# Written order through the last attention chunk, later routing, a third plane buffer, and one load issued from ScalarE, in a fused attention and mixture-of-experts kernel

## The chip, the cores and the metric

The kernel runs on one core of a Trainium2 chip. The metric is the device time of one execution in microseconds; three runs of the kernel before gave 1425.99, 1426.38 and 1427.35 us, so the median is 1426.38 us.

## The reference

For each of 8 batches of 1856 rows, attention without a softmax, multiplied by `u`; the 14848 rows that come out go through a mixture of 16 experts (4 groups of 4), of which each row visits one.

```python
scores = (1.0 / S) * np.matmul(z, z.transpose(0, 2, 1))    # z: 8 x 1856 x 64
attn = np.maximum(scores, 0.0) ** 2
x = (u * np.matmul(attn, v)).reshape(B * S, D)             # D = 256
...
g_idx = np.argmax(x @ w_group, axis=1)                     # a group of four
e_idx = np.argmax(xg @ w_expert[g], axis=1)                # an expert in it
h = np.maximum(xg[mask_e] @ w1[g, e], 0.0)                 # 256 -> 1024
out[tok_idx] = (g_w * e_w)[:, None] * (h @ w2[g, e])       # 1024 -> 256
```

## The kernel before

**Attention.** A batch is cut into four chunks of queries (512, 512, 512 and 320 columns in the batches that matter here), and a chunk into 15 steps, one for each block of 128 keys. The steps of the whole kernel are numbered s = 0 to 479; batch 7, the last, has steps 420 to 479, its third chunk is 450 to 464 and its fourth, the last of all, 465 to 479. I write (7,2) for the third chunk of batch 7, counting from 0. In every turn of the main loop (`for s in range(NS)`) the kernel writes, in this order: loads and splits of operands that are due, `scores(s + 6)`, `attn_v(s)`, at a chunk's last step `chunk_end(s)`, then the deferred work that is due (`run_deferred`), then a few instructions of routing (`run_gens`). `scores` makes the two operands `ah` and `al` of a step, high and low part of the squared scores; `attn_v` is six matmuls on them. So the operands are written six steps ahead of their use.

The score matrix of a batch is symmetric. A key block that an earlier chunk has computed transposed is not computed again: `put_mirror` stores it to DRAM (`sym`), `load_mirror` brings four blocks back into one tile `at` (three buffers) with four DMAs on SyncE's queue, seven steps ahead, and `scores` only splits it: a ScalarE copy `ah<-at` (line 359) and a VectorE subtraction `al<-at,ah` (line 360). In the last chunk 12 of 15 blocks come that way, in three loads; the other three (keys 12 to 14) are computed.

**The end of a chunk.** `chunk_end` multiplies the sums by `u` into `xT` (one buffer), splits `xT` into `xh` (ScalarE, `split_x`) and `xl` (VectorE, `rest_x`), copies it as 16-bit planes into `pl` (`planes`, ScalarE, line 465), from which four DMA transposes on SyncE's queue make rows, computes the router's logits (four matmuls `pl<-xh,whl` and `pl<-xl,wh`, lines 483 and 484) and brings these through `lgp` and a DMA transpose to `lgx`. Each piece is due a number of steps after the chunk: `XO` for the split, `LG` for the logits, `PL` for the planes. `pl` has two buffers (line 116), which `load_x` also uses for the rows that an expert reads back (`xp`).

**Routing.** `route` is a generator of small dependent VectorE instructions for two chunks together, or for one chunk each at the end: 12 or 13 of them lead to a pair of small matmuls (`pk`, lines 610 and 611) that rank the rows by expert; from these come the row addresses `di`, and one indirect DMA on GpSimd's queue per 128 rows scatters the rows to `bucket` in DRAM. The generators run one after the other, 5 instructions a step in the last chunk and 4 a turn behind it. A `yield` with a number waits so many steps. `wait` (line 507) says how long after its chunk a route starts: 15 for chunks (7,0) and (7,1) together, 8 for (7,2), 5 for (7,3). Four times in a route an instruction is wrapped in `pin`: it may not be placed ahead of what its engine was given just before in the written order. One of the pinned ones is the first `pk` matmul.

**Experts.** Expert blocks 0 and 1 are the first 512 rows of two experts and read rows that were scattered long before. A block is `phase1` (48 matmuls, eight groups of six) and `phase2_t` (48 matmuls). Between the groups of blocks 0 and 1, `early` runs one turn of the deferred work and of the routing: eight turns in `phase1`, two in `phase2_t`. After `phase1` of block 1, `while deferred or gens: early(i)` writes out all that is left. Block 2 reads rows that the last scatters write: its load `xp<-bucket` waits for all of them, then `join_x` makes `xf`, `xh_m`, `xl_m`.

**Order.** Instructions are put in order on each engine by a planner with its own model of time, which takes the written order as priority among what it holds ready. Between steps 15 and 465 a region holds TensorE, ScalarE and VectorE to the written order; behind it the planner is free. SyncE and GpSimd are the planner's throughout this stretch.

```python
def early(i):
    run_deferred(late["at"])
    run_gens(late["at"], 4)
    late["at"] += 1
    more_rows(i)
...
pin(nc.tensor.matmul(pk[:, 0:W], tri, ohf, start=True, stop=True))
```

## Time and profile before

| | us |
|---|---|
| median of three runs | 1426.38 |
| the profiled execution | 1423.95 |
| its span, first to last instruction | 1422.1 |
| TensorE busy | 1411.9 |
| VectorE busy | 1216.5 |
| ScalarE busy | 1051.3 |

The span is what one execution's instructions cover; the profiled execution's own time is 1.85 us more. A busy TensorE here is one with a matmul in its pipeline; whether the next matmul came as soon as it could is read from the distances between the starts in the timeline. Names in a row are the tiles of the program, out<-in.

### The profile page before, as it was taken

How to read it: one execution, taken by the hardware profiler on the slowest of the kernel's cores; microseconds unless marked ns; L12 is line 12 of the kernel's file. 1: busy time of each engine (PE TensorE's matmuls, PEld its weight loads, DVE VectorE, ACT ScalarE, POOL GpSimd, SP SyncE). 2: the span in 40 equal slices, each digit the busy share in tenths (PEclk: the TensorE clock that was granted, in tenths of full speed). 3: DMA queues.
4: the chain of work that ended last, by engine and by line, in shares of the span. 5: the costliest groups of instructions: out<-in, count | busy, mean ns of one | idle time of the engine just before them, and what ended most of it. 6: DMA issues, size and time to landing. Idle time of an engine off the chain costs nothing.

```text
span 1422.1 us, 22589 instructions
## 1 busy us (share of the span) xinstructions
PE 1411.9 (99%) x7010; PEld 1223.8 (86%) x7010; DVE 1216.5 (86%) x2436; ACT 1051.3 (74%) x1849; POOL 439.0 (31%) x462
## 2 busy tenths in 40 slices
PE   9999999999999999999999999999999999999998
PEld 7898888888888888888878898988888888899997
DVE  7889999899998999998988667789777888888884
ACT  8887887787887878878776354357777777777773
POOL 0002022220222012202222331332445555555554
PEclk9999999999999999999999999999999999999999
DMA  9997979979899698895987564534555444555552
GB/s 318 328 260 210 235 187 254 230 192 239 195 262 238 160 264 207 223 244 151 243 197 165 116 142 113 122 82 130 126 136 132 126 123 113 138 137 136 139 140 60
DMA packets 400043, 256.47 MB, mean 180 GB/s; under 512 B 244131, under 2 KB 355262, under 8 KB 399920
## 3 DMA queue, kind: packets, MB, share of 16 engines
q1 hardware_dynamic: 387984, 223.97, 63.1%
q0 software_dynamic: 11856, 30.90, 7.7%
q8 instruction: 56, 0.92, 0.3%
q14 instruction: 67, 0.55, 0.1%
q10 hardware_dynamic: 80, 0.13, 0.0%
HBM read 108.29 MB, written 89.21 MB: 139 GB/s over the span
## 4 chain that ended last, share of the span: by engine, by line
PE 92%; DVE 2%; DMA 2%; issue 2%; POOL 1%; ACT 1%; SPq 0%; POOLq 0%; DVEq 0%; ACTq 0%
PE o L408 38%; PE duo_p L887 15%; PE yT L887 6%; PE duo_y L1333 6%; PE sc L370 5%; PE sc L371 5%; PE ph L802 2%; PE ph L803 2%; PE ph L804 2%; PE duo_w L1333 2%; PE duo_x L1333 2%; PE duo_p L1333 2%; PE duo_z L1333 2%; PE pl L483 1%; PE pl L484 1%
## 5 line engine op out<-in xcount | busy, mean ns | idle before, releaser
L408 PE MATMUL o<-ah,vl 128*128 128x512 f32 (+2 forms) x960 | 354.6, 370 | 0.4 <-DVE ah L382 0.4
L408 PE MATMUL o<-ah,vh 128*128 128x512 f32 (+2 forms) x960 | 354.2, 369 | 0.0
L408 PE MATMUL o<-al,vh 128*128 128x512 f32 (+2 forms) x896 | 328.7, 369 | 0.9 <-DVE al L360 0.9
L646 POOL DMA_INDIRECT bucket<-rows,di x121 | 138.6, 1145 | 383.3 <-issue 216.7
L374 ACT ACTIVATE r<-sc 128x512 f32<-128x512 f32 (+2 forms) x312 | 178.8, 573 | 74.4 <-PE sc L371 72.8
L408 PEld LDWEIGHTS o<-ah,vl 128*128 128x128 f32 x960 | 180.2, 188 | 31.0 <-DVE ah L382 1.2
L408 PEld LDWEIGHTS o<-ah,vh 128*128 128x128 f32 x960 | 180.2, 188 | 28.9
L385 DVE TENSOR_TENSOR al<-r,ah 128x512 fp32r<-128x512 f32 (+2 forms) x280 | 187.7, 671 | 19.1 <-ACT r L379 2.2
L930 POOL DMA_INDIRECT out_dram<-y_w,meta_w x92 | 139.3, 1514 | 191.4 <-ACT y_w L924 145.8
L408 PEld LDWEIGHTS o<-al,vh 128*128 128x128 f32 x896 | 167.8, 188 | 27.5 <-DVE al L360 1.2
L887 PE MATMUL duo_p<-hh_w,duo_w 128*128 128x496 f32 (+10 forms) x692 | 178.0, 371 | 0.0
L381 ACT ACTIVATE r<-r 128x512 f32<-128x512 f32 (+2 forms) x280 | 171.4, 612 | 8.9
L887 PEld LDWEIGHTS duo_p<-hh_w,duo_w 128*128 128x128 f32 x692 | 128.6, 188 | 16.7
L382 DVE CAST ah<-r 128x512 fp32r<-128x512 f32 (+2 forms) x280 | 115.9, 414 | 18.8 <-ACT r L381 13.4
L370 PE MATMUL sc<-zm,z2h 128*128 128x512 f32 (+2 forms) x312 | 120.0, 385 | 0.2 <-DVE zm L251 0.2
L371 PE MATMUL sc<-zm,z2l 128*128 128x512 f32 (+2 forms) x312 | 118.9, 381 | 0.0
L310 DVE STREAM_TRANSPOSE mt<-r 128x512 f32<-128x512 f32 x147 | 103.6, 705 | 0.6
L887 PE MATMUL duo_p<-hl_w,duo_w 128*128 128x496 f32 (+10 forms) x346 | 104.1, 371 | 0.0
L360 DVE TENSOR_TENSOR al<-at,ah 128x512 fp32r<-128x512 f32 (+1 forms) x168 | 95.3, 579 | 2.5 <-ACT ah L359 2.3
L359 ACT CAST ah<-at 128x512 fp32r<-128x512 f32 (+1 forms) x168 | 86.1, 531 | 8.8 <-DMA at<-sym 3.9
L807 ACT ACTIVATE hh<-ph 128x512 fp32r<-128x512 f32 (+6 forms) x96 | 45.7, 488 | 39.4 <-PE ph L804 38.6
L887 PE MATMUL yT<-hh,w_e 128*128 128x512 f32 (+6 forms) x352 | 74.1, 328 | 0.0
(259 smaller groups left out, 2874.5 us busy)
## 6 DMA issues: line engine op xcount, KB each, us to landing
sym<-mt SPq DMA_DIRECT2D x126, 256.0 KB
duo_r<-in_w_dram SPq DMA_DIRECT2D x48, 512.0 KB
at<-sym SPq DMA_DIRECT2D x84, 256.0 KB
bucket<-padrow SPq DMA_DIRECT2D x32, 660.0 KB
at<-sym SPq DMA_DIRECT2D x84, 160.0 KB
vr<-in_v_dram SPq DMA_DIRECT2D x23, 512.0 KB
ut<-in_uT_dram SPq DMA_DIRECT2D x23, 512.0 KB
raw_e<-in_w_dram SPq DMA_DIRECT2D x16, 512.0 KB
```

What stands on the lines that cost most here:

```text
L310: nc.vector.transpose(out=t2.rearrange("p (j t x) -> p t j x", t=KT, x=32), in_=a.rearrange("p (t j x) -> p t j x", t=KT, x=32))
L370: held(nc.tensor.matmul(ps[:, 0:w], z2h[:, ks], zm, start=True, stop=False))
L371: held(nc.tensor.matmul(ps[:, 0:w], z2l[:, ks], zm, start=False, stop=True))
L374: held(nc.scalar.activation(out=a, in_=ps[:, 0:w], func=AF.Relu, scale=1.0 / S))
L381: held(nc.scalar.activation(out=a, in_=a, func=AF.Square))
L382: held(nc.vector.tensor_copy(out=ah, in_=a))
L385: held(nc.vector.tensor_sub(out=al, in0=a, in1=f32(ah)))
L408: held(nc.tensor.matmul(oa[d][:, 0:QW[b][c]], (vh if q else vl)[:, d0:d0 + P], al if q == 2 else ah, start=(i == 0 and q == 0), stop=end a ...
L646: nc.gpsimd.indirect_dma_start(out=views[(b * NQ + 2 * half + hs[h]) * NT + i], out_offset=bass.IndirectOffsetOnAxis(ap=di[0:n, i0 + i:i0 ...
L887: nc.tensor.matmul(o, wt["2"][f // 2][:, w0:w0 + P], hs[f][q // 2][:, c0:c0 + n], start=(at == 0), stop=(at == 3 * NF - 1))
L930: nc.gpsimd.indirect_dma_start(out=outs(), out_offset=bass.IndirectOffsetOnAxis(ap=meta[0:m, t, 1:2], axis=0), in_=y[0:m], in_offset=None, ...
L1333: nc.tensor.matmul(out, a, b, start=(q == 0 and m in (1, 5)), stop=(q == 2), skip_group_check=True)
```

## The change

- `pl` has three buffers instead of two.
- The last of the three loads of the last chunk, `(7, 2, 3)`, is issued from ScalarE's queue instead of SyncE's.
- The last chunk takes its keys in another order: 12 and 14 come two steps and one step later, 3 a step earlier, 13 a step later.
- The region of written order ends at step 479 instead of 465. With it, `not last` takes the place of `s + 1 < NS - NK` for chunk (7,2): its split comes 2 steps after the chunk instead of at once, its planes 3 and 4 instead of 1 and 2, its logits 9 instead of 2.
- Logits of chunk (7,1) come 9 steps after the chunk instead of 7; planes stay at 9. The split of (7,0) comes one step sooner.
- The route of (7,0) and (7,1) starts 23 steps after (7,1) instead of 15: at step 472 instead of 464.
- Weight pieces of expert 0 are loaded and split in the order 0, 1, 2, 3, the last two later. The rows of block 0 are loaded three steps later and joined three steps later.
- In the last expert's second half, one output tile has a buffer of its own; the others share `y`.

```diff
--- before.py
+++ after.py
@@ -113,7 +113,7 @@
         return sb("rows", [P, 4, RW], I32, 4, name)
 
     def new_pl(name):
-        return sb("pl", [P, 2048], U16, 2, name)
+        return sb("pl", [P, 2048], U16, 3, name)
 
     def new_xhl(name):
         return tuple(new_vb(f"{h}_{name}").rearrange("p (d q) -> p d q", d=ND) for h in ("xh", "xl"))
@@ -321,9 +321,10 @@
 
         g = QW[b][cc] // 32
         at = new_at(f"at_{b}_{c}_{cc}").rearrange("p (g x) -> p g x", x=P)
+        eng = nc.scalar if (b, c, cc) == (B - 1, 2, NQ - 1) else nc.sync
         src = sym.pop((b, c, cc))[0:g * 32, :].rearrange("(g r) (j x) -> j r g x", r=32, x=P)
         for j in range(4):
-            nc.sync.dma_start(at[j * 32:(j + 1) * 32, 0:g, :], src[j])
+            eng.dma_start(at[j * 32:(j + 1) * 32, 0:g, :], src[j])
         ats[(b, c, cc)] = at[:, 0:g, :].rearrange("p g (t x) -> p t g x", t=KT)
 
     steps = [(b, c, i) for b in range(B) for c in range(NQ) for i in range(NK)]
@@ -336,7 +337,7 @@
 
     def key(b, c, i):
         if (b, c) == (B - 1, NQ - 1):
-            return (0, 1, 12, 2, 3, 14, 4, 5, 13, 6, 7, 8, 9, 10, 11)[i]
+            return (0, 1, 2, 3, 12, 4, 14, 5, 6, 13, 7, 8, 9, 10, 11)[i]
         return KORD[c][i] if MB[0] <= b < MB[1] else i
 
     NS = len(steps)
@@ -495,16 +496,16 @@
                 lgx.rearrange("p t h l -> p (t h) l"), lgp[:, 0:nt].rearrange("p t h q -> p (t h q)")
             )
 
-        LG = (7 if b == B - 1 and c < 2 else (9 if c == 2 else 8 if c == 0 else 7)) if s + 1 < NS - NK else 2
-        XO = 2 if s + 1 < NS - NK else 0
+        LG = (7 + 2 * c if b == B - 1 and c < 2 else (9 if c == 2 else 8 if c == 0 else 7)) if not last else 2
+        XO = (1 if (b, c) == (B - 1, 0) else 2) if not last else 0
         (split_x() if XO == 0 else defer(s + XO, split_x))
         (rest_x() if XO == 0 else defer(s + XO + 1, rest_x))
-        PL = XO + 1 if not XO or c == 2 else LG + 2
+        PL = XO + 1 if not XO or c == 2 else LG + (0 if (b, c) == (B - 1, 1) else 2)
         defer(s + PL, lambda: planes(0))
         defer(s + PL + 1, lambda: planes(1))
         defer(s + LG, logits)
         defer(s + LG + (1 if XO else 0), logits_out)
-        wait = 5 if last else 12 if b == 0 and c < 2 else (17 if c == 1 and b < B - 1 else 15) if s + 1 < NS - NK else 8
+        wait = 5 if last else 12 if b == 0 and c < 2 else (17 if c == 1 and b < B - 1 else 23 if b == B - 1 else 15) if s + 1 < NS - NK else 8
         alone = b == B - 1 and c >= NQ - 2
         if c % 2 or alone:
             gens.append((max(s + wait, PFILL[-1] + 2), route(b, c // 2, (c % 2,) if alone else (0, 1))))
@@ -839,7 +840,7 @@
             for f in range(0 if pair else NF):
                 w2t = wt["2"][f // 2][:, (f % 2) * 512:(f % 2 + 1) * 512]
                 held(nc.tensor.matmul(py[0:m, 0:D], hs[f][1][:, ts], w2t[:, 0:D], start=False, stop=(f == NF - 1)))
-            y = sb("yl", [P, D], F32, 3, f"y_{name}_{t}")
+            y = sb(*(("yl", [P, D], F32, 1) if one else ("y", [P, D], F32, 3)), f"y_{name}_{t}")
             cw = meta[0:m, t, 0:1].bitcast(F32)
             top = py[0:m, 0:D]
             if pair:
@@ -987,7 +988,7 @@
             s0 = (b - 1) * NQ * NK
             begin.setdefault(s0 + load[0] * NK + load[1], []).append((what, b, n))
             split_at.setdefault(s0 + cut[0] * NK + cut[1], []).append((what, b, n))
-    WPREP = ((2, (2, 3), (2, 9)), (0, (2, 4), (2, 12)), (1, (2, 5), (2, 14)), (3, (3, 0), (3, 6)))
+    WPREP = ((0, (2, 3), (2, 12)), (1, (2, 4), (2, 14)), (2, (2, 5), (3, 2)), (3, (3, 6), (3, 11)))
     xs = []
     ahead = 4
     for s in range(ahead):
@@ -1002,7 +1003,7 @@
         b, c, k = steps[s]
         if s == NK:
             region.enter_context(tc.manual_schedule(engines={mybir.EngineType.PE, mybir.EngineType.Activation, mybir.EngineType.DVE}))
-        if s == NS - NK:
+        if s == NS - 1:
             region.close()
         if s in (1, 4):
             pz.pop(0)()
@@ -1029,11 +1030,11 @@
             prep.pop((what, n))()
         if k == (5 if s < NK else 5) and nxt < B * NQ:
             prep_zm(nxt // NQ, nxt % NQ)
-        if s == NS - NK - 6:
+        if s == NS - NK - 3:
             load_rows(0)
         if s == NS - 6:
             load_rows(1)
-        if s == NS - 12:
+        if s == NS - 9:
             xs.append(join_x(0, rows_b[0][0], blocks[0][2]))
         while ahead < min(NS, s + LEAD + 1, max(4, 3 + s + s // 2)):
             scores(ahead)
```

## Rows read from the trace of the kernel before

**Rows 1.** Page, part 1: busy us (share of the span) and instructions of each engine.

```profile
PE 1411.9 (99%) x7010; PEld 1223.8 (86%) x7010; DVE 1216.5 (86%) x2436; ACT 1051.3 (74%) x1849; POOL 439.0 (31%) x462
```

**Rows 2.** TensorE's waits, whole span: us in total, times, longest.

```profile
PE pl L484 <- DVE xl L441: 1.3, 1, 1.3
PE o L408 <- DVE al L360: 0.9, 1, 0.9
```

**Rows 3.** TensorE timeline, step 456: start us, us, engine line op out<-in [idle <-releaser].

```profile
728.49 0.40 PE L483 MATMUL pl<-xh,whl 128*48 128x512 f32 x1
730.14 0.44 PE L484 MATMUL pl<-xl,wh 128*48 128x512 f32 x1 [1.26 <-DVE xl L441]
```

**Rows 4.** VectorE timeline beside it, two merged.

```profile
729.35 1.34 DVE L441 TENSOR_TENSOR xl<-xT,xh 128x512 fp32r<-128x512 f32 x2
```

**Rows 5.** TensorE timeline in the last chunk.

```profile
751.88 0.31 PE L408 MATMUL o<-ah,vl 128*128 128x320 f32 x1
752.03 0.31 PE L408 MATMUL o<-ah,vh 128*128 128x320 f32 x1
753.28 0.56 PE L408 MATMUL o<-al,vh 128*128 128x320 f32 x2 [0.94 <-DVE al L360]
```

**Rows 6.** ScalarE's waits from 740 to 756 us: total, times, longest.

```profile
ACT pl L465 <- DMA rows<-pl: 3.0, 1, 3.0
...
ACT ah L359 <- DMA at<-sym: 0.2, 1, 0.2
```

**Rows 7.** SyncE timeline, 735 to 750 us: DMA issues.

```profile
735.75 5.06 SPq L767 DMA_TRANSPOSE xp<-bucket  x1
...
742.21 5.14 SPq L471 DMA_TRANSPOSE rows<-pl  x4
747.45 2.03 SPq L326 DMA_DIRECT2D at<-sym  x4
```

**Rows 8.** VectorE timeline ahead of the second stop.

```profile
751.29 1.33 DVE L781 COPY xf<-xp 128x2048 uint16<-128x2048 uint16 x1
...
752.74 0.89 DVE L360 TENSOR_TENSOR al<-at,ah 128x320 fp32r<-128x320 f32 x2
```

**Rows 9.** ScalarE timeline: the one DMA that it issues before.

```profile
0.80 0.56 ACTq L241 DMA_DIRECT2D zr<-in_zT_dram  x1
```

**Rows 10.** Windows view, last chunk: length, busy PE, PEld, DVE, ACT, POOL; clock, DMA, GB/s.

```profile
745.00:765.00 20.00, 19.06 (x110) 16.85 (x109) 16.54 (x47) 11.35 (x21) 0.54 (x2) 1.00 0.85 168
```

**Rows 11.** TensorE timeline: block 1 starts, last rank, phase2_t, block 2 starts.

```profile
781.16 0.39 PE L802 MATMUL ph<-xh_m,w1l_e 128*128 128x512 f32 x1
...
788.05 0.20 PE L610 MATMUL pk<-oh,tri 128*128 128x64 bf16 x1
...
792.48 0.84 PE L887 MATMUL yT<-hh,w_e 128*128 128x512 f32 x3
...
803.36 0.33 PE L802 MATMUL ph<-xh_m,w1l_e 128*128 128x384 f32 x1
```

**Rows 12.** VectorE timeline: the last addresses, block 2's join.

```profile
790.13 0.22 DVE L623 TENSOR_REDUCE di<-rk 128x4 int32<-128x64 f32 x1
...
799.63 1.04 DVE L781 COPY xf<-xp 128x1536 uint16<-128x1536 uint16 x1 [3.39 <-DMA xp<-bucket]
```

**Rows 13.** GpSimd timeline: the last chunk's three scatters.

```profile
791.12 0.95 POOL L646 DMA_INDIRECT bucket<-rows,di  x1 [2.68 <-issue]
...
793.65 0.90 POOL L646 DMA_INDIRECT bucket<-rows,di  x1 [0.30 <-issue]
```

**Rows 14.** SyncE and ScalarE timelines: block 2's load, its split.

```profile
795.96 1.45 SPq L767 DMA_TRANSPOSE xp<-bucket  x1
...
800.71 0.83 ACT L786 CAST xh_m<-xf 128x768 fp32r<-128x768 f32 x1 [7.43 <-DVE xf L781]
```

**Rows 15.** VectorE and TensorE timelines: the rank of (7,2), ready and run.

```profile
774.21 0.56 DVE L598 TENSOR_TENSOR pre<-pre,oh 128x16 bf16<-128x16 bf16 x3
...
779.08 0.20 PE L610 MATMUL pk<-oh,tri 128*128 128x64 bf16 x1
```

## The prediction, made before the changed kernel was seen

> **What bounds the kernel now.** I read the page first: TensorE is busy for 1411.9 of 1422.1 us [rows 1], so only what TensorE loses can be won. The list of its waits [rows 2] then names two that lie near the change, and its timeline says what each is worth, as the distance between two starts less the usual distance. The first: in step 456 the logits of (7,1) start at 728.49 and their second product at 730.14, 1.65 us later where 0.23 is usual (48 products take 11.32 us [rows 11]), so 1.42 us are lost; the releaser is `xl` [rows 3], which VectorE makes from 729.35 to 730.69 [rows 4]. The second, in the last chunk: 752.03 to 753.28 is 1.25 us where the products before it lie 0.15 apart, so 1.10 us are lost, on an `al` [rows 5].
>
> The second has its cause further back. ScalarE waited 3.0 us for row transposes to leave a `pl` buffer, and only 0.2 us for a mirrored load [rows 6]. These transposes, four in 5.14 us, were issued behind a load of block 0's rows that held SyncE's queue for 5.06 us; the third mirrored load came behind both, at 747.45 [rows 7]. With `pl` of two buffers, (7,2)'s planes need the one that (7,1)'s rows are read from. ScalarE's copies behind the wait came late, and VectorE was then inside the 1.33 us join of block 0's rows when the `al` was wanted [rows 8].
>
> Then I read what follows the attention, since the change moves the routing into it. Block 1 starts at 781.16, its second half at 792.48 and block 2 at 803.36 [rows 11]. Block 2 needs rows that the last scatters write: the last rank matmul runs at 788.05 [rows 11], `di` is done at 790.35 [rows 12], three scatters start from 791.12 to 793.65 and end at 794.55 [rows 13], the load is issued at 795.96 [rows 14], `xf` starts at 799.63 [rows 12] and `xh_m` ends at 801.54 [rows 14]. That is 1.82 us ahead of TensorE. This slack is the number that decides.
>
> **The change part by part.** *Logits of (7,1) two steps later.* Two steps are 12 products of 0.23, 2.7 us; the wait is 1.4, and the second `xl` ends at 730.69 [rows 4] where the logits would begin at about 731.2. All 1.42 us go. *Third plane buffer.* (7,2)'s planes find a free buffer, the 3.0 us on ScalarE go [rows 6], and with them the 1.10 us. Together **-2.52**.
>
> *Written order in the last chunk.* Its 90 products at 0.15, with scores and logits, are some 14.5 us of TensorE. In the 20 us from 745 VectorE is busy for 16.54 and ScalarE for 11.35 [rows 10]; what of this belongs to block 0's results and to (7,2)'s route now falls behind the chunk, so VectorE has about 14 us of work for 14.5, with six steps (5.3 us) of lead as cover. If the cover is gone, TensorE waits for an `al` near the end: between 0 and 16.54 - 14.5 = 2.0. I take +0.2, nearer to nothing, because the route's 13 instructions are written at steps 472 to 474, behind most of the operands. Block 0 no longer fills in, but nothing is left to fill.
>
> *Mirrored load on ScalarE.* Four issues took 2.03 us on SyncE [rows 7]; ScalarE's only one took 0.56 [rows 9]. So ScalarE loses 2.0 to 2.2 us, and before that it waits for the `at` buffer, until VectorE has subtracted key 3 (now a step sooner, so that this read is written ahead of the load): some 0.45 to 1.33, a subtraction or a join [rows 8]. Queued behind it are `scores(469)` and its copies; VectorE and then TensorE wait for those, 5.3 us later. Covered, 0; the load's own lateness cost 0.2 on ScalarE at most.
>
> *Weight pieces, block 0's rows, the split of (7,0), the output buffers.* Pieces and rows are used behind step 480; the join at step 471 leaves nine steps, 7.9 us, for three instructions of up to 1.33 [rows 8]. 0 each; a missing output buffer in the tail would cost one scatter's pitch, 1.27.
>
> *Routing eight steps later.* This is the term with a price. The generators run in turn, so I count instructions. Before: the route of (7,0) and (7,1) starts at 464 and ranks at 476; (7,2) ranks in turn 487, (7,3) in turn 494, which is behind group 4 of block 1, 30 products after its start. The row agrees: 788.05 is 6.89 us behind 781.16 [rows 11]. After: start 472, thirteen instructions and the gap of 9, so the first rank falls in turn 483; eleven more instructions; (7,2) reaches its gap of 5 in turn 489 and ranks in turn 494, where (7,3) ranked before; (7,3) is started in turn 497 and written out behind group 7. Its rank is pinned there, so it can't run ahead of the second half of block 1, at +11.32 from block 1's start (792.48 - 781.16).
>
> From (7,2)'s rank at +6.89 to its first scatter are 3.07 us (791.12 - 788.05) [rows 11, 13], so +9.96. Scatters start every 1.27 us [rows 13]; (7,2) has four and (7,3) three behind them. The fifth starts at +15.0, which is later than what the pin allows (11.32 + 3.07 = +14.4), so GpSimd's queue decides; the seventh ends at +18.45. From there to the end of `xh_m` were 6.99 us (794.55 to 801.54) [rows 13, 14], so +25.44. TensorE is there at +22.20 (803.36 - 781.16). It waits **3.24 us**. From below: the rank's two matmuls could lie closer and save some 0.8, so 2.4. From above: the planner put (7,2)'s rank at 779.08 although its input was done at 774.77 [rows 15], 4.3 us late; the same on (7,3) gives a rank at +15.6, scatters from +18.7 to +22.1, `xh_m` at +29.1 and a wait of 6.9. I take 3.24: VectorE has less else to do there.
>
> In the stretch with a TensorE idle of 0.94 us the granted clock was 1.00 [rows 10], the 2.4 GHz level, and no row shows a wait of three. The Trainium skill ("TensorE: Matmul & The Clock Gate", What's actually happening) says that an idle TensorE goes back to half clock and is released by activity. By the rows the wait costs itself alone; by the page some products of block 2 would run at half speed as well, which is the fourth rival.
>
> *Sum.* -2.52 + 0.2 + 3.24 = **+0.9** on the profiled execution's 1423.95 (span 1422.1 and 1.85 around it): 1424.9. It lies 2.43 under the median of the runs, which I carry over: 1426.38 + 0.9 = **1427.3**.
>
> **The rivals.** *The wait at block 2 stays away* (rank and scatters run early, or VectorE's chain is much shorter): -2.52 + 0.2, 1424.1. For it, planner and hardware disagree on times; against it, the pin and seven scatters in one queue. *Late rank*, on the slower side: the planner places (7,3)'s rank inside block 1's second half. It decides from a wait of 5.2 us on, a rank 2 us behind +11.32 plus the 0.6 us that the scatter queue hides; at the 4.3 us of rows 15 the sum is -2.52 + 0.2 + 6.9 = +4.6, 1431.0. For it, one such lateness in the rows; against it, little competes with the rank there. *VectorE is too full in the last chunk*, or ScalarE's issues outlast the lead: 2.0 instead of 0.2, so +2.7, 1429.1. For it, 16.54 of 20 us; against it, 5.3 us of lead. *The clock falls in the wait*: a 384-column product takes about 0.18 us at 2.4 GHz (from 0.15 for 320 columns, rows 5) and twice that at 1.2 GHz; eleven of them give +2.0, so +2.9 in all, 1429.3.
>
> **How the numbers follow.** Forecast 0.55 (1426.3 to 1428.5, with a wait of 2.4 to 4.0 and 0 to 0.6 in the chunk), no wait 0.12, late rank 0.14, full VectorE 0.12, clock 0.07. A measurement here tells 0.2% from no change, 2.85 us: faster is below 1423.5, slower above 1429.2. Faster needs "no wait" and more than its own 2.3 us: 0.06. Slower takes most of the late rank and half of the next two: 0.24. The rest, 0.70, is the same. The range, 1424.2 to 1431.0, cuts most of the first rival's lower side and what is later than the late rank.
>
> **What would show it.** TensorE's waits no longer list `pl` on `xl` nor the 0.9 us on `al`; ScalarE has no wait for `rows<-pl`, and its timeline has four DMA issues. `phase1` of block 0 starts only when the attention is through, and block 1 starts some 2.5 us sooner than before. The rank of (7,2) follows group 4 of block 1 and that of (7,3) its group 7; seven scatters follow each other without a gap; and block 2's first product waits about 3 us for `xh_m`. The prediction is wrong if block 2 follows block 1 without a wait, or if a new wait of over 1 us stands in the last chunk.

## The result and the profile after

| | before | after |
|---|---|---|
| median | 1426.38 (1425.21 to 1427.69) | 1440.40 (1438.68 to 1443.14) |
| profiled execution, and its span | 1423.95, 1422.1 | 1440.31, 1438.5 |
| TensorE busy | 1411.9 | 1419.9 |

The changed kernel is 14.0 us slower, ratio 1.0099 (1.0088 to 1.0110). The forecast was 1427.3, in a range of 1424.2 to 1431.0, so it was 13 us too low. In a second comparison the step was 11.8 us (run a1_again, below).

From line 324 on, each line of the code stands one lower than before, so L409 is the former L408. TensorE's waits after the change, to be read against [rows 2] (engine and line, whom it waited for, us in total, times, longest):

```profile
PE ph L803 <- ACT xh_m L787: 5.1, 1, 5.1
PE o L409 <- DVE ah L383: 3.0, 2, 2.7
PE yT L888 <- ACT hh L808: 2.0, 1, 2.0
...
PE o L409 <- DVE ah L389: 0.5, 1, 0.5
PE o L409 <- DVE al L361: 0.5, 1, 0.5
```

The two waits that were to go are gone, `pl` on `xl` and the 0.9 us on `al`. New ones took their place at three points: ahead of block 2 (`ph` on `xh_m`), in the last chunk (`o` on `ah` and `al`; 0.4 of the 3.0 is the start of the kernel) and in block 1 (`yT` on `hh`). The profile of a1_again has no row for the third, and its span is 4.2 us shorter. In the first trace 96 of the 1656 updates of TensorE's semaphore are missing, in a1_again's none; whether the stop in block 1 has to do with that, and whether the other four executions of the first comparison had it, isn't shown. It is left out from here on, so some 2 us of the 14.0 stay unexplained.

**The last chunk.** TensorE's timeline there, and the windows around it (busy time and instructions of PE, PEld, DVE, ACT and POOL, then granted clock, share of the DMA engines, GB/s):

```profile
748.24 0.42 PE L409 MATMUL o<-ah,vl 128*128 128x320 f32 x1 [2.65 <-DVE ah L383]
...
750.48 0.64 PE L409 MATMUL o<-al,vh 128*128 128x320 f32 x1 [0.48 <-DVE al L361]
750.91 0.47 PE L409 MATMUL o<-ah,vl 128*128 128x320 f32 x1
...
752.43 0.64 PE L409 MATMUL o<-ah,vl 128*128 128x320 f32 x1 [0.52 <-DVE ah L389]
```

```profile
740.00:745.00 5.00, 5.00 (x33) 4.77 (x32) 0.00 (x0) 0.00 (x0) 0.00 (x0) 1.00 1.34 175
...
750.00:755.00 5.00, 4.00 (x14) 3.61 (x15) 4.93 (x11) 4.22 (x9) 0.00 (x0) 0.55 0.65 142
755.00:760.00 5.00, 5.00 (x26) 4.44 (x26) 3.71 (x7) 2.98 (x5) 0.31 (x1) 0.77 0.49 123
```

From 740 to 745 TensorE works alone: VectorE and ScalarE do nothing at all. It lives on the six steps of lead, and then stops three times. Behind the stop of 2.65 us the clock is granted at 0.55 and 0.77 in the two windows, and products of 320 columns start 0.26 us apart (750.91 and the next, 751.17) and not 0.15.

Why both engines stood still is in the queues of ScalarE and SyncE. In such a row the second number of a DMA issue covers the whole of the merged issues:

```profile
737.13 0.45 ACT L360 CAST ah<-at 128x320 fp32r<-128x320 f32 x1
741.49 5.35 ACTq L327 DMA_DIRECT2D at<-sym  x4
746.89 0.44 ACT L375 ACTIVATE r<-sc 128x320 f32<-128x320 f32 x1 [9.30 <-DMA rows<-pl]
```

```profile
733.31 1.11 SPq L327 DMA_DIRECT2D at<-sym  x2
734.88 0.41 SPq L771 DMA_DIRECT2D meta<-bucket  x1
736.59 5.27 SPq L768 DMA_TRANSPOSE xp<-bucket  x1
741.98 5.13 SPq L472 DMA_TRANSPOSE rows<-pl  x4
```

ScalarE is idle for 9.30 us, and what ends it is named as `rows<-pl`, a transfer of SyncE with which the load has nothing to do. The semaphores that the trace records with each DMA tell why. A transfer counts up one of eight semaphores when it lands, and in this stretch SyncE's and ScalarE's transfers use the same eight in turn. The waits recorded with ScalarE's four issues name the semaphore that each will count on itself, so each waited until the transfer that had used it before had landed:

| ScalarE's issue | the transfer before on its semaphore, issued by SyncE | its last count |
|---|---|---|
| 741.49 | a mirrored piece of the load before, 733.31 | 741.40 |
| 742.24 | `meta`, 734.88 | 742.22 |
| 743.98 | `xp`, 736.59 | 743.96 |
| 746.51 | first row transpose, 741.98 | 746.49 |

Four of four agree within 0.1 us. So ScalarE got in line behind SyncE's transfers after all; only now its squaring and splitting, on which VectorE and then TensorE live, stood in that line too. Not all of the line is the 5.3 us load of block 0's rows: the first 3.9 of the 9.30 us ended with the landing of a mirrored piece that SyncE had issued ahead of that load. It took 8.1 us to land, and from 734 us on the busy share of the DMA engines was 1.00 or more. The Trainium skill ("DMA: Bandwidth & Descriptors", Why a DMA increments its semaphore by 16 and not by 1) asks for one semaphore for each transfer in flight, because the counts of a second one can let a wait for the first pass too early; the table agrees with it, as no issue there came before the earlier transfer on its semaphore had landed. The Trainium skill says in another section of that page, "Issuing engines are not separate DMA queues", that issuing from several engines only saves the time of the issue itself; here it cost the issuing engine 9.30 us.

**Block 2**, in a1_again. TensorE's ranks of (7,0) with (7,1), of (7,2) and of (7,3), block 1's first product, the end of block 1 and block 2's first products; GpSimd's first scatter of (7,0), its last of (7,2) and its first of (7,3); VectorE's last inputs of the first and the last rank, and its wait for the last; and the clock:

```profile
784.20 0.23 PE L611 MATMUL pk<-oh,tri 128*128 128x128 bf16 x1
...
785.29 0.40 PE L803 MATMUL ph<-xh_m,w1l_e 128*128 128x512 f32 x1
...
792.20 0.20 PE L611 MATMUL pk<-oh,tri 128*128 128x64 bf16 x1
...
799.80 0.20 PE L611 MATMUL pk<-oh,tri 128*128 128x64 bf16 x1
...
807.54 0.39 PE L888 MATMUL yT<-hl,w_e 128*128 128x512 f32 x1
813.62 0.69 PE L803 MATMUL ph<-xh_m,w1l_e 128*128 128x384 f32 x1 [5.68 <-ACT xh_m L787]
814.11 0.52 PE L804 MATMUL ph<-xh_m,w1h_e 128*128 128x384 f32 x1
```

```profile
787.23 1.09 POOL L647 DMA_INDIRECT bucket<-rows,di  x1 [19.20 <-DVE sm L629]
...
801.27 0.97 POOL L647 DMA_INDIRECT bucket<-rows,di  x1 [0.30 <-issue]
802.96 0.95 POOL L647 DMA_INDIRECT bucket<-rows,di  x1 [0.72 <-issue]
```

```profile
768.62 0.18 DVE L602 TENSOR_TENSOR pre<-pre 128x64 bf16<-128x64 bf16 x1
...
796.80 0.15 DVE L599 TENSOR_TENSOR pre<-pre,oh 128x16 bf16<-128x16 bf16 x1
...
801.31 0.23 DVE L615 TENSOR_TENSOR rk<-pk,base 128x64 f32<-128x64 f32 x1 [3.16 <-PE pk L612]
```

```profile
810.00:815.00 5.00, 1.38 (x4) 1.38 (x5) 2.39 (x4) 0.83 (x1) 0.00 (x0) 0.59 0.87 180
815.00:820.00 5.00, 5.00 (x23) 5.00 (x23) 3.19 (x8) 0.88 (x2) 3.41 (x4) 0.72 0.62 139
```

Block 1 starts at 785.29 here, so the rank of (7,3) stands at +14.51. Its input was ready at 796.95, +11.66: in TensorE's order it stands 2.85 us later. The rank of (7,0) and (7,1) is later still: its input was ready at 768.80, and it runs at 784.20, 15.4 us after that and 1.09 ahead of block 1. So their eight scatters start only at 787.23, and with those of (7,2) they keep GpSimd's queue full, 0.3 us between one and the next, until 802.24. The first scatter of (7,3) starts at 802.96; had its rank been early, the queue would have let it start at about 802.5. The late rank and the full queue thus end within some 0.4 us of each other, and either alone would have made block 2 wait. Why the planner put the two ranks where they are isn't shown. TensorE stops for 5.68 us, and block 2's first twelve products run at half clock (granted 0.59 in the first of these windows; 0.5 is the 1.2 GHz level).

**A ledger.** For each trace I took the distances between TensorE's starts, subtracted from each the median distance of products of that line and shape in the same trace, and summed what is left over 20 us at a time. That gives the time that TensorE lost, stops and slow clock together, in three stretches that matter: 720 to 740 (the logits of (7,1)), 740 to 760 (the last chunk) and 800 to 820 (the start of block 2). The first stretch of block 0, 760 to 780, is added where it holds something. The last two columns are the medians against the kernel before on the same chip in the same comparison. The four columns before them come from one execution, the profiled one, and the medians from 4 to 11, so where the executions of a kernel spread (e6 from 1426.1 to 1429.9, e9 from 1423.4 to 1425.4, b3 from 1425.6 to 1429.4) the two needn't agree.

| kernel | 720 | 740 | 760 | 800 | us against before | ratio, 95% |
|---|---|---|---|---|---|---|
| before | 1.6 | 1.4 | 0.3 | 0.0 | | |
| after, as a1_again | 0.0 | 7.2 | 0.0 | 8.0 | +11.8 | 1.0083 (1.0066 to 1.0099) |
| e1_load_on_sync | 0.0 | 3.5 | 0.1 | 8.1 | +7.9 | 1.0054 (1.0038 to 1.0071) |
| e2_route_at_15 | 0.0 | 9.9 | 0.9 | 0.0 | +7.3 | 1.0050 (1.0033 to 1.0067) |
| e3_both | 0.0 | 9.0 | 1.1 | 0.0 | +5.7 | 1.0039 (1.0024 to 1.0053) |
| e4_rows_behind | 0.0 | 1.9 | 8.4 | 6.4 | +15.2 | 1.0109 (1.0092 to 1.0126) |
| e5_load_on_gpsimd | 0.0 | 0.0 | 0.2 | 8.2 | +4.8 | 1.0034 (1.0022 to 1.0047) |
| e6_gpsimd_wait20 | 0.1 | 5.7 | 1.9 | 1.6 | +4.2 | 1.0025 (1.0016 to 1.0035) |
| e7_no_scatter | 0.0 | 0.0 | 0.2 | 8.3 | +5.1 | 1.0037 (1.0022 to 1.0052) |
| e8_end_465 | 0.1 | 6.9 | 0.2 | 0.0 | +2.5 | 1.0018 (1.0009 to 1.0028) |
| e9_gap6 | 0.1 | 0.0 | 0.2 | 4.0 | -0.9 | 0.9996 (0.9987 to 1.0006) |
| e10_gap4_2 (its stop is at 782.93) | 0.1 | 0.0 | 0.2 | 0.0 | +2.7 | 1.0021 (1.0012 to 1.0030) |
| e11_gap6_4 | 0.0 | 0.0 | 0.2 | 2.4 | -0.4 | 0.9998 (0.9989 to 1.0008) |
| b1_pl_lg | 0.0 | 2.4 | 0.3 | 0.0 | -1.2 | 0.9991 (0.9981 to 1.0000) |
| b2_pl_lg_gpsimd | 0.0 | 4.9 | 0.2 | 0.0 | +1.8 | 1.0017 (1.0008 to 1.0026) |
| b3_gpsimd_only | 1.6 | 6.4 | 0.4 | 0.0 | +2.9 | 1.0023 (1.0013 to 1.0032) |
| b4_written | 1.8 | 6.5 | 0.1 | 0.0 | +4.0 | 1.0034 (1.0024 to 1.0044) |
| b5_key_join | 0.1 | 6.7 | 1.8 | 0.0 | +6.0 | 1.0045 (1.0031 to 1.0058) |
| b6_pl_only | 1.7 | 0.8 | 0.4 | 0.0 | -0.8 | 0.9994 (0.9985 to 1.0004) |

In a1_again the three stretches gained 1.6 and lost 5.8 and 8.0, together 12.2, which is the difference of the spans (1434.3 to 1422.1).

### The profile page after: what moved, and what is told of

It is laid out like the page before. It is cut to its first block, busy times and chain, and to the rows that moved or that the text cites. A ratio compares the mean times of both kernels' runs of the same rounds, so it can differ in the third digit from the quotient of the medians.

```text
span 1438.5 us, 22567 instructions
## 1 busy us (share of the span) xinstructions
PE 1419.9 (99%) x7010; PEld 1230.2 (86%) x7010; DVE 1217.5 (85%) x2436; ACT 1047.6 (73%) x1849; POOL 432.8 (30%) x462
## 4 chain that ended last, share of the span: by engine, by line
PE 91%; DVE 2%; issue 2%; DMA 2%; POOL 2%; SPq 1%; ACT 0%; POOLq 0%; another core or an unknown queue 0%; DVEq 0%; ACTq 0%
PE o L409 38%; PE duo_p L888 14%; PE duo_y L1334 6%; PE yT L888 5%; PE sc L371 5%; PE sc L372 5%; PE ph L803 2%; PE ph L804 2%; PE ph L805 2%; PE duo_w L1334 2%; PE duo_x L1334 2%; PE duo_p L1334 2%; PE duo_z L1334 2%; PE pl L484 1%; PE pl L485 1%
## 5 line engine op out<-in xcount | busy, mean ns | idle before, releaser
L409 PE MATMUL o<-ah,vl 128*128 128x512 f32 (+2 forms) x960 | 356.0, 371 | 3.6 <-DVE ah L383 3.0
L409 PE MATMUL o<-ah,vh 128*128 128x512 f32 (+2 forms) x960 | 355.6, 371 | 0.0
L409 PE MATMUL o<-al,vh 128*128 128x512 f32 (+2 forms) x896 | 331.7, 371 | 0.5 <-DVE al L361 0.5
L647 POOL DMA_INDIRECT bucket<-rows,di x121 | 134.7, 1113 | 387.9 <-issue 215.8
L409 PEld LDWEIGHTS o<-ah,vl 128*128 128x128 f32 x960 | 181.2, 189 | 34.8 <-DVE ah L383 4.0
L409 PEld LDWEIGHTS o<-ah,vh 128*128 128x128 f32 x960 | 181.2, 189 | 29.0
L409 PEld LDWEIGHTS o<-al,vh 128*128 128x128 f32 x896 | 169.0, 189 | 26.9 <-DVE al L361 0.7
```

The source lines that it names most:

```text
L409: held(nc.tensor.matmul(oa[d][:, 0:QW[b][c]], (vh if q else vl)[:, d0:d0 + P], al if q == 2 else ah, start=(i == 0 and q == 0), stop=end a ...
L647: nc.gpsimd.indirect_dma_start(out=views[(b * NQ + 2 * half + hs[h]) * NT + i], out_offset=bass.IndirectOffsetOnAxis(ap=di[0:n, i0 + i:i0 ...
```

## The experiments

**a1_again**: the changed kernel, unaltered.

> The changed kernel, unaltered, looked at a second time. If ScalarE's 5.07 us before the last hh of block 1 (and TensorE's 2.3 us stop there) belong to the first profiled execution alone, this profile has neither, the rest of its trace is as before, and its span is 2 to 4 us shorter; if they belong to the kernel, both are there again. The stop of 2.8 us in the last chunk and of 5.3 us ahead of block 2 should be there in either case. Against the kernel before: 1.009 to 1.011.

The stop in block 1 was gone, the two others stayed (2.5 and 5.7 us in the list of waits), and the median was 1435.98 where the kernel before took 1424.19.

**e1_load_on_sync, e2_route_at_15, e3_both.** The third load goes back to SyncE, the routing back to 15 steps, and both.

```diff
-        eng = nc.scalar if (b, c, cc) == (B - 1, 2, NQ - 1) else nc.sync
+        eng = nc.sync
```

```diff
-        wait = ... 23 if b == B - 1 else 15) ...
+        wait = ... 15) ...
```

> The changed kernel with one part undone: the third mirrored load is issued by SyncE again; key order, written order and late routing stay. Theory A (ScalarE's four issues stood behind SyncE's transfers, and this is what stopped TensorE in the last chunk): ScalarE's idle stretch of 9.30 us at 737.6 falls below 4, TensorE's 2.82 us stop and the clock of 0.55 behind it go, and with them 6 to 8 us of the 14: 1432.4 to 1434.4. Rival (the written order is what starves TensorE there, VectorE and ScalarE having no block 0 to fill in with): a stop of over 2 us stays in the last chunk, 1438 to 1441.

> The changed kernel with one other part undone: the routing waits 15 steps again and not 23; the load stays on ScalarE. Theory B (the late routing alone makes block 2 wait 5.3 us and run its first products slowly): TensorE's stop for xh_m at block 2 falls below 1 us and the clock there is 1.00, the last chunk stays as it is, 1431 to 1434. Rival (block 2 waits because the whole of the last chunk ran late, and the routing with it): the stop stays above 3 us, 1438 to 1441.

> Both of these parts undone; left of the change are the third plane buffer, the logits of (7,1) two steps later, the key order, the written order through the last chunk and the moved weight pieces. If the two losses add up and the gains of 1.4 and 1.1 us are as predicted: 1423 to 1425, under the kernel before. If the written order or the key order costs as well: 1426 to 1430. If the two losses hide one another, so that either one alone brings most of the 14 us: e1 and e2 each stay above 1436 and this one is at 1424 to 1427.

e1: 3.6 of the 7.2 us went, about half of what was expected, and the clock stayed at 1.00 up to block 2. The rest is a stop of 1.5 us on the load itself, which SyncE issues at 747.33, and one of 1.6 ahead of block 0. e2: the stop ahead of block 2 is gone, as theory B had it; the last chunk lost 2.7 us more. e3: block 2 doesn't wait and the load is on SyncE, yet 9.0 us are lost in the last chunk. So the parts don't add up; a further wait comes up as soon as these two go. VectorE's timeline names it, in e3:

```profile
742.78 1.28 DVE L431 TENSOR_TENSOR xT<-o,ut 128x512 f32<-128x512 f32 x2
749.17 0.53 DVE L549 COPY lgf<-lgx 128x640 uint16<-128x640 uint16 x1 [5.11 <-DMA lgx<-lgp]
```

The first instruction of the route waits 5.1 us for the transposed logits of (7,1), and the splits of the last chunk are queued behind it. In the trace of the kernel before, SyncE issued that transpose ahead of the rows' four [rows 7]; with the logits two steps later it comes behind them, at 746.72 here. b6 and b1 below show this one edit at work. Before:

```profile
740.91 1.19 SPq L494 DMA_TRANSPOSE lgx<-lgp  x1
```

**e4_rows_behind**: ScalarE issues as in the changed kernel, but SyncE's load of block 0's rows comes later.

```diff
+        ins = nc.sync.dma_start_transpose(xp[:, :, 0:n], bucket16[ds(r0, n), 0:2 * D])
+        if name == 0:
+            tc.keep_in_program_order(ins)
...
-        if s == NS - NK - 3:
+        if s == NS - NK + 1:
             load_rows(0)
...
-        if s == NS - 9:
+        if s == NS - 2:
             xs.append(join_x(0, rows_b[0][0], blocks[0][2]))
```

> The changed kernel with the third load still on ScalarE, but SyncE's 5.3 us load of block 0's rows is kept behind the transposes of (7,1)'s rows, and its join at step 478. Theory A in its narrow form (each of ScalarE's issues waits until the earlier transfer that shares its completion semaphore has landed, and these were two mirrored pieces, the meta load, the rows load and the first row transpose): the idle stretch of ScalarE falls from 9.3 to 3.5 to 5 us, with the same four issues on the same queue, the stop of 2.8 us in the last chunk falls below 1, and the time to 1433 to 1437 (block 0's first product may wait 1 to 2 us for its rows). Rival 1 (issuing on ScalarE costs by itself, or it waits for the buffer): the idle stretch stays at 8 to 10 us, 1439 to 1442. Rival 2 (the weight pieces fill the transfer queues and hold everything until 742): the idle stretch ends where it did, within 1 us of the landing at 741.4 plus the issues, and comes to 5 to 6 us.

```profile
738.83 3.64 ACTq L327 DMA_DIRECT2D at<-sym  x4
742.52 0.44 ACT L375 ACTIVATE r<-sc 128x320 f32<-128x320 f32 x1 [5.02 <-PE o L409]
```

The idle stretch fell from 9.30 to 5.02 us with nothing changed on ScalarE. Its length alone doesn't decide, since the narrow theory gave 3.5 to 5 us and rival 2 gave 5 to 6. The single issues do: here too the second to fourth (740.99, 741.34, 742.14) stand within 0.15 us behind the last count of the transfer before on their semaphore (740.97, 741.21, 742.12); the first (738.83) stands 0.43 behind. Rival 2 is right in part: the second issue waited for a mirrored piece that SyncE had issued at 733.18, and its lateness has nothing to do with the load of block 0's rows, which now comes at 743.83. The stop in the last chunk fell to 1.1 us and not below 1. The time was missed: 1439.48, since block 0 waited 6.6 us for its rows, where I had allowed 1 to 2.

**e5_load_on_gpsimd, e7_no_scatter.** The load is issued by GpSimd; in e7 the eight scatters of (7,0) and (7,1) are left out as well.

```diff
-        eng = nc.scalar if ...
+        eng = nc.gpsimd if ...
```

```diff
-            for i in range(nt):
+            for i in range(0 if (b, half) == (B - 1, 0) else nt):
```

> The changed kernel with the third mirrored load issued by GpSimd, which has nothing to do between 731 and 782: it stands neither in ScalarE's queue nor behind SyncE's transposes. Theory A: no stop over 0.6 us in the last chunk, ScalarE has no idle stretch over 4 us there; against the kernel with the load on SyncE the 1.5 us stop at 753 goes as well, block 2 still waits 5 to 6 us: 1429 to 1431 on a chip where the kernel before takes 1424.3. Rival (what GpSimd waits for ends only with the load of block 0's rows, about 741 to 744, so that the load lands as late as on SyncE): the stop of 1.5 us stays, 1431 to 1433.

> The changed kernel with the load on GpSimd, and without the eight scatters of (7,0) and (7,1): their rows are missing in the output. These eight stood in GpSimd's queue ahead of the seven of (7,2) and (7,3), and the prediction had left them out. If the queue sets the end of the last scatter, TensorE's wait ahead of block 2 falls from 5.9 us to 3.0 to 3.6; if the rank of (7,3), 14.5 us behind block 1's start, sets it, the wait falls by at most 0.5 us; if the rank comes earlier without them, its distance from block 1's start says so.

In e5 GpSimd issues at 738.40 and nothing is lost in the last chunk, with the written order, the key order, the third buffer and the late routing all in place. TensorE's list of waits holds, but for the start of the kernel, only block 2's:

```profile
PE ph L803 <- ACT xh_m L787: 5.8, 1, 5.8
```

So all of the last chunk's 7.2 us hang on where the load is issued. GpSimd's four transfers count on four other semaphores, whose earlier transfers had landed by 725.9. e7 leaves the wait ahead of block 2 where it was, 5.9 us. The scatters of (7,2) then start at 788.08, +9.89 behind block 1's start (778.19), those of (7,3) with a gap before them:

```profile
791.99 0.96 POOL L647 DMA_INDIRECT bucket<-rows,di  x1 [0.30 <-issue]
795.83 1.12 POOL L647 DMA_INDIRECT bucket<-rows,di  x1 [2.87 <-issue]
```

GpSimd is idle for 2.87 us and then starts 3.1 us behind the rank of (7,3), at 792.70 (+14.51). Without the eight scatters the rank sets the end, and the wait is as long, so emptying the queue alone doesn't help. The other test, an early rank with the eight scatters still ahead, wasn't run.

**e6_gpsimd_wait20, e9_gap6, e10_gap4_2, e11_gap6_4.** On e5: the routing at 20 steps; or at 23 with shorter pauses ahead of the ranks, in turns: 6 for (7,0) and (7,1), 4 with 2 for (7,2), 6 with 4.

```diff
-        yield {(B - 1, 1, 0): 5, ...}.get((b, half, hs[0]), 9 if half or b == B - 1 else 7)
+        yield {(B - 1, 1, 0): 5, ...}.get((b, half, hs[0]), (6 if b == B - 1 else 9) if half or b == B - 1 else 7)
```

> The same, with the routing of (7,0) and (7,1) at step 469 (waiting 20 steps and not 23). At 15 steps VectorE stood 5.1 us in the last chunk for the transposed logits of (7,1), which land at about 749, in the written order; at step 469 it reaches them about then. Three turns earlier, the rank of (7,3) lies some 4 us ahead of +14.5 behind block 1's start, so the wait ahead of block 2 falls from 5.9 to 1 to 3 us and the time to 1425 to 1428. Rival 1 (VectorE's order holds TensorE in the chunk again): a stop over 1 us on VectorE's ah there, 1428 to 1431. Rival 2 (the planner puts the rank where it likes in block 1): the wait stays above 4 us, 1429 to 1431.

> The changed kernel with the load on GpSimd, and the pause ahead of the rank of (7,0) and (7,1) six turns long and not nine. By the count of turns the rank of (7,3) comes three turns, some 3 to 4 us, earlier: at +10.5 to +11.5 behind block 1's start, and the wait ahead of block 2 falls from 5.9 to 1 to 2.5 us with the clock there at 1.00; the last chunk stays free of stops: 1422 to 1424 where the kernel before takes 1424.4. Rival (VectorE's chain for (7,3) is what is late): the wait stays above 4 us, 1428 to 1430.

> The same with pauses of four turns ahead of the rank of (7,0) and (7,1) and two (not five) ahead of that of (7,2). The rank of (7,3) then stands 34 products behind block 1's first, before its second half, about +7: no wait ahead of block 2, no stop in the last chunk, and all of the 3.0 us that the kernel before loses between 720 and 760 gone: 1421 to 1422.5, 2 to 3 us under the kernel before. Rival (TensorE reaches these ranks before VectorE has their input): a stop of 1 to 3 us in block 0 or block 1 for a pk, 1423 to 1426.

> The changed kernel with the load on GpSimd, pauses of six turns ahead of the rank of (7,0) and (7,1) and four ahead of that of (7,2). The rank of (7,3) stands 50 products behind block 1's first, where it stood 53 with six and five: 0.5 to 0.8 us earlier, so the wait ahead of block 2 falls from 2.3 to 1.5 to 1.8 us. In the other runs stops of up to 1.6 us left the clock at 1.00; if this one does too, the 4.0 us lost there fall to under 2: 1421 to 1423 where the kernel before takes 1424.4, 1.5 to 3 us under it. Rival (the rank of (7,2) comes before VectorE has its input): TensorE waits for it in block 1, 1423.5 to 1425.

e6 (1428.41): the wait ahead of block 2 fell to 1.5 us as expected, but the route's instructions came ahead of the join of block 0's rows on VectorE (`xf` at 754.95), and block 0 started 3.3 us late. e9: the rank of (7,0) and (7,1) ran 0.23 us behind its input, 16.1 us ahead of block 1 and not 1.1, so their scatters had ended before (7,2)'s began; the rank of (7,3) stood at +11.30 instead of +14.51, the wait fell to 2.3 us, and the time to 1423.59, inside the expectation. The run took away both limits at once. The clock there was to be 1.00; in the trace it fell. e11: the rank of (7,3) was to come 0.5 to 0.8 us earlier still; it came at +11.32, no earlier, and the stop stayed at 2.28 us. e10: the rank of (7,2) went ahead of block 1, and VectorE stood for the next transposed logits, with `xf` of block 1 behind them:

```profile
777.85 0.46 DVE L549 COPY lgf<-lgx 128x320 uint16<-128x320 uint16 x1 [3.31 <-DMA lgx<-lgp]
...
780.39 1.41 DVE L782 COPY xf<-xp 128x2048 uint16<-128x2048 uint16 x1
```

TensorE waited 4.3 us for block 1's `xh_m`; 1427.18, worse than either rival.

**e8_end_465, b4_written**: the written order alone. e8 is e3 with the region ending at step 465 again; b4 is the kernel before with the region ending at 479.

```diff
-        if s == NS - 1:
+        if s == NS - NK:
             region.close()
```

> The run with load and routing both undone, with one more part undone: the written order ends at step 465 as in the kernel before. Kept of the change: third plane buffer, logits of (7,1) two steps later, key order, weight pieces, block 0's rows and join three steps later. If the written order is what stops VectorE for 5.1 us and TensorE for 4.2 (9.0 us lost between 740 and 760), this stretch loses under 2.5 us and the kernel is within 1.5 us of the kernel before or up to 2.5 under it. If key order or pieces are the cause, 6 to 9 us stay lost there and it is 4 to 6 us slower.

> The kernel before with one edit: the written order of TensorE, VectorE and ScalarE ends at step 479 and not at 465. The prediction gave it 0.2 us, 2.0 at most. Theory now, from the run with load and routing both undone: the routing of (7,0) and (7,1), written at step 464, stops VectorE until the transposed logits have landed at about 748, so TensorE stops 3 to 5 us in the last chunk, its clock falls to about half behind it, and the kernel is 4 to 8 us slower than before. Rival (what cost there was the key order or the moved weight pieces): 0 to 2 us slower.

e8 still loses 6.9 us in the last chunk (2.5 us slower than before, where 4 to 6 was expected with such a loss), so the written order isn't most of what e3 suffers from; VectorE stands as in e3:

```profile
749.10 0.53 DVE L549 COPY lgf<-lgx 128x640 uint16<-128x640 uint16 x1 [5.10 <-DMA lgx<-lgp]
```

The later logits alone don't do this. b1 has them too, with the order ending at 465 and the routing at step 464, and there VectorE has other work until the logits are nearly in (0.26 us of wait) and the chunk loses 2.4 us. Which of the parts that e8 has beyond b1 (key order, weight pieces, block 0's rows, the later split of (7,2)) empties VectorE's queue wasn't separated.

b4 is 4.0 us slower, the size that I gave, but not by the mechanism: VectorE has no idle stretch over 2 us there, and the loss is four stops of 0.5 to 1.6 us, on `xh` and `xl` of (7,2)'s logits, on an `ah` and on block 0's `xh_m`, with a clock of 0.50 behind the last.

**b1_pl_lg, b6_pl_only, b5_key_join, b2_pl_lg_gpsimd, b3_gpsimd_only**, on the kernel before. b6 is the third plane buffer (with the output tile's buffer) alone, b1 adds the logits and planes of (7,1), b5 to that the key order and the join at step 471, b2 to b1 the load on GpSimd, and b3 is the load on GpSimd alone.

```diff
-        return sb("pl", [P, 2048], U16, 2, name)
+        return sb("pl", [P, 2048], U16, 3, name)
...
-        LG = (7 if b == B - 1 and c < 2 else ...
+        LG = (7 + 2 * c if b == B - 1 and c < 2 else ...
-        PL = XO + 1 if not XO or c == 2 else LG + 2
+        PL = XO + 1 if not XO or c == 2 else LG + (0 if (b, c) == (B - 1, 1) else 2)
```

> The kernel before with two parts of the change alone: three plane buffers (with the output tile taken from the pool of the other outputs, for room) and the logits and planes of (7,1) two steps later. By the prediction's first two terms 1.42 and 1.10 us go: 2.0 to 2.6 us under the kernel before. Rival (the 1.10 us hang on SyncE's queue, where the load of block 0's rows and the transposes stand ahead of the third mirrored load in any case): only the 1.4 us go, and ScalarE or VectorE wait for that load instead: 0.8 to 1.6 under it. If the freed buffer lets a later load in earlier and that delays the mirrored load: no gain or a loss of up to 2.

> The kernel before with three plane buffers alone. The 1.6 us lost between 720 and 740 on the logits of (7,1) stay. By the prediction the 1.10 us stop in the last chunk goes: 0.9 to 1.3 us under the kernel before. Theory now: ScalarE's 3.0 us wait goes, but the third mirrored load, still behind SyncE's transposes, is then waited for, and VectorE's join stands where it stood: 0 to 1.1 us above the kernel before, with a stop on the load in the list.

> The kernel before with three plane buffers, logits and planes of (7,1) two steps later, the changed key order of the last chunk (the third load's keys fifth, seventh and tenth) and the join of block 0's rows at step 471. With planes and logits alone, 1.03 us were lost on the third load and 1.14 on an al behind the join. If these are the causes, TensorE loses at most 0.6 us between 740 and 760 and the kernel is 2.2 to 3.0 us under the kernel before. If the planner places the work otherwise, one stop of about 1 us stays and it is 0.8 to 2 under it.

> The kernel before with three plane buffers, the logits of (7,1) two steps later and the third mirrored load issued by GpSimd; order and routing as before. In the run with the first two alone a stop of 1.03 us on this load (ScalarE's ah) and one of 1.14 on an al stood in the last chunk. If the 1.10 us of the prediction hung on SyncE's queue and not on the plane buffer, the stop on the load goes, the one on al shrinks with it, and of the 3.0 us that TensorE lost between 720 and 760 at most 1 is left: 2.0 to 2.9 us under the kernel before. Rival (VectorE's join of block 0's rows alone makes the al late): 1.1 us stay there, 1.6 to 2.0 under it. If GpSimd's load crowds something out: no gain.

> The kernel before with one edit: the third mirrored load is issued by GpSimd. If the 1.10 us of the last chunk hang on SyncE's queue, they go although the plane buffers stay two: 0.8 to 1.3 us under the kernel before, and ScalarE's 3.0 us wait for the row transposes may stay. If they hang on the plane buffer as predicted, the stop of 1.1 us stays: within 0.4 of the kernel before.

b6: the 1.1 us stop became one of 0.66 on the load; the time is 0.8 us lower, which can't be told from none. b1: the 1.6 us of the logits went, and two stops came up in the last chunk; the time is 1.2 us lower, in the rival's range:

```profile
PE o L408 <- DVE al L360: 1.0, 1, 1.0
PE o L408 <- ACT ah L359: 0.9, 1, 0.9
```

SyncE's queue shows the price of the later logits. First b6, then b1:

```profile
741.39 1.19 SPq L494 DMA_TRANSPOSE lgx<-lgp  x1
742.68 5.15 SPq L471 DMA_TRANSPOSE rows<-pl  x4
```

```profile
742.01 5.14 SPq L471 DMA_TRANSPOSE rows<-pl  x4
747.25 1.22 SPq L494 DMA_TRANSPOSE lgx<-lgp  x1
748.56 2.03 SPq L326 DMA_DIRECT2D at<-sym  x4
```

The transposed logits come 5.9 us later, and the load behind them 1.1 us later than before [rows 7]. b2, b3 and b5 all missed: GpSimd's load, free in e5, made the kernel before slower. It is issued later there, at 744.22 in b2 and 743.21 in b3, and the waits recorded with it name semaphores of SyncE's, of which the last counts, at 744.2 and 743.1, belong to a row transpose and to the load of block 0's rows; in e5 the last of SyncE's was at 737.6. So a load on GpSimd can stand behind SyncE's transfers too. In b3 ScalarE waits for the row transposes with its copy into `pl`, in b2 VectorE for the transposed logits, in b5 ScalarE for the load and then for a weight piece that SyncE issued behind block 1's rows:

```profile
752.54 1.04 ACT L465 COPY pl<-xT 128x1024 uint16<-128x1024 uint16 x1 [6.22 <-DMA rows<-pl]
```

```profile
751.84 0.53 DVE L548 COPY lgf<-lgx 128x640 uint16<-128x640 uint16 x1 [2.33 <-DMA lgx<-lgp]
```

```profile
756.21 0.62 ACT L202 CAST w_e<-raw_e 128x512 fp32r<-128x512 f32 x1 [3.16 <-DMA raw_e<-in_w_dram]
```

Whether ScalarE's load with the old key order would do better wasn't tried. No kernel here beats the one before by more than a measurement tells.

## Why the prediction was wrong

- **Logits of (7,1), -1.42: right in its place, half of the account.** The stretch goes from 1.6 to 0.0 us in every run that has the edit. What I left out: the transpose of these logits passes behind the rows' four in SyncE's queue, 5.9 us later, and a route that starts early can then wait for it on VectorE (5.1 us in e3 and e8, 2.3 in b2, 0.3 in b1). I had moved the four matmuls and not the DMA that follows them.
- **Third buffer, -1.10: half of the mechanism, and too large.** ScalarE no longer waits for `rows<-pl`, but the load behind the same queue is late by itself, which the prediction read as 0.2 us on ScalarE at most, with the longer wait in front of it: in b6 a stop of 0.66 on the load is left, and TensorE wins 0.6 us.
- **Written order, +0.2:** with the load on GpSimd nothing is lost in the last chunk (e5), so the term stands in that setting. By itself, on the kernel before, it costs 5.1 us there (b4). A price for the written order without the rest of the change would have been wrong.
- **Load on ScalarE, 0: the step that failed first.** I took 2.0 to 2.2 us for the issues and 0.45 to 1.33 for the buffer, 3.5 at most, under a lead of 5.3. The four issues held ScalarE for 9.30, since each also waited for an earlier transfer of SyncE on its semaphore. On SyncE the four came so late that these had landed, so the rows of before don't show that wait; the order of the transfers and SyncE's 5.06 us [rows 7] were there to be read. The loss is 7.2 us of TensorE, of which 4.2 are stops (2.70, 0.65 and 0.84 by the distances) and 3.0 slow clock.
- **Late routing, +3.24: the right wait, the size of a rival.** TensorE lost 8.0 us. The rank of (7,2) stood at +6.91, as counted (+6.89). Two steps failed. First, the rank of (7,0) and (7,1), counted for turn 483, inside block 0's first half, ran 1.09 us ahead of block 1, so eight scatters that the count of seven leaves out filled GpSimd's queue. With them the prediction's own figures (3.07 us from rank to scatter, 1.27 from one to the next, 6.99 to the end of `xh_m`) give a wait of about 5.4 us, an estimate from [rows 11, 13, 14] and the measured rank. Second, the rank of (7,3) was to be pinned behind group 7, at +11.32, and stood at +14.51, 2.85 us behind its input. That is the late rank, which I had given 0.14 and 6.9 us, with 4.3 us of lateness taken from [rows 15]. Each of the two holds block 2 up by nearly the whole wait of 5.7 us: e7 shows it for the rank, and for the queue it is worked out from the rows above. The queue was a right reason, but with too few scatters in it.
- **The clock: a rival with 0.07 that came true, and in the last chunk as well.** At block 2 it took 8.0 - 5.85 = 2.1 us (5.85 is the stop by the distances of the starts), and 2.0 was its price; in the last chunk 3.0 more. No row of before gives the eleven slow products behind that price; twelve ran slowly here, so its closeness is in part luck. The Trainium skill ("TensorE: Matmul & The Clock Gate", What's actually happening) says that an idle TensorE goes back to half clock; the granted 0.55 and 0.59 behind these two stops agree.
- **The sum.** By the ledger, against the forecast: -1.6 for -1.4; +5.8 in the last chunk for -0.9; +8.0 at block 2 for +3.2. Of the 11.3 us that the forecast missed by this trace, 6.7 are ScalarE's issue and 4.8 the late routing (late ranks and full queue together), each with its slow clock; 0.2 go the other way. The 13 us of the first comparison hold some 2 more, which no trace settles.
- **What was to be seen:** right were the vanished waits, ScalarE's four issues, block 0 behind the attention, and the rank of (7,2). Wrong were block 1's earlier start (785.29 for 781.16 before, 4.1 us later and not 2.5 sooner), the rank of (7,3), and the size of block 2's wait. The new wait of over 1 us in the last chunk, named as what would make the prediction wrong, is what did.

## What to carry to other kernels

A DMA that is moved to a computing engine's queue brings its waits with it: list the transfers that use its completion semaphore before it, and when they land, before calling the issue covered. Of a matmul that is moved, follow its output through the transfer queue to the engine that waits for it in order; in e3 and e8 one later transpose put 5 us on VectorE. When work is moved later, count what it pushes into a queue ahead of the work that decides; here eight scatters. A stop of TensorE of the lengths seen here is to be priced with slow products behind it: where the clock fell, they cost 1.5 to 3 us on top.

## What the hardware showed

- Every stop of TensorE from 2.6 to 6.8 us was followed by a granted clock of about 0.5. Below that the length alone doesn't tell. Stops of 1.5 and 1.6 us, 2.8 us apart, left it at 1.00 in e1, while 1.1 and 1.6 us, as far apart, brought it to 0.50 in b4. Two stops ahead of block 2, 2.31 us in e9 and 2.28 in e11, went either way; the windows behind them, first e9, then e11:

```profile
805.00:807.50 2.50, 2.50 (x11) 2.50 (x9) 1.04 (x3) 0.00 (x0) 1.89 (x3) 0.56 0.62 155
```

```profile
805.00:807.50 2.50, 2.50 (x17) 2.50 (x16) 1.88 (x5) 0.98 (x2) 1.98 (x2) 1.00 0.61 156
```

That stop cost 4.0 us in one and 2.4 in the other. It seems to go either way from one execution of the same kernel to the next, by their times and mean clocks (0.999 in the shorter ones, 0.998 in the longer): of e9's ten, seven took 1423.4 to 1423.9 us and three, the traced one among them, 1425.0 to 1425.4; of e11's eleven, eight, the traced one among them, took 1423.5 to 1423.9 and three 1424.8 to 1425.1.
- Four small loads by GpSimd took 2.52 us to issue (from 738.40), against 2.03 on SyncE [rows 7], and landed from 742.7 to 747.5 beside SyncE's transposes (e5).
